# Two sequence mixers side by side: 2048-point transforms factored as 32 by 64 in place of 16 by 128

## The chip, the cores and the metric

The kernel runs on one core of a Trainium2 chip. Its engines are PE (matrix products; its weight loads are shown as PEld), DVE (elementwise work and scans), ACT (here mostly copies of PE's results out of PSUM), POOL (some integer work, and the issue of some transfers) and SP (the issue of the others). The metric is the device time of one execution in microseconds. Three runs of the kernel before gave 219.19, 219.22 and 219.26 us.

## What is computed

Two independent blocks take sequences of 2048 steps and 640 channels and write halves of one output row. Block A is a diagonal complex state-space layer, block B a gated long convolution (H3):

```python
# A: complex state per channel p
h = Lam_bar[None, :] * h + Bu[:, t, :]              # Bu = x @ B_bar.T, for t = 0 .. 2047
y = 2.0 * einsum("blp,dp->bld", hseq, Cmat).real + x * Dskip
# B
k_shift = sum over 4 taps of k_pad[:, t:t + S, :] * shift_k[:, 3 - t]
kv = k_shift * v
y = irfft(rfft(kv, 2S) * rfft(ssm_k, 2S))[:, :S] + kv * ssm_D
out = q * y
concatenate([A, B], axis=-1)                        # (1, 2048, 1280), bf16
```

## The kernel before

**Block A** works through four chunks c of 512 steps and, in each, five tiles j of 128 state channels; n = 5c + j. `z{n}` is ten matmuls of 512 columns (L356), `ze{n}` ACT's copy of the result. On DVE `rin{n}` turns the phase away with three tensor operations (`rotate`, L367 to L369), `sc{n}` scans the real and the imaginary part (L376) and `rout{n}` turns back (L367 to L369 again). `p{c}_{i}_{j}` projects tile j of 128 rows (L401, four matmuls of 320 columns; at j = 4 six more with the skip weights, L407), `yo` is ACT's copy (L411), `yd` the store (L415). `la` (POOL, L385) and `carry` (DVE, L390 to L392) hand the state to the next chunk.

**Block B** works through five groups G of 128 channels. `kT`, `vT` load k and v transposed, `dS` builds diagonal weights (L447), `tap` makes the short convolution on PE (L462), `kve` copies, `kv` multiplies by v on DVE (L473). `kvo` stores the product to DRAM and `kvs` loads it back as 128 rows of (channel in a set, coarse step) with one run of neighbouring steps each (`load_kv`, L478); `hs` loads the long filter in the same form, and `had` adds the skip coefficient to its first step (L444). Both go through a transform in two stages, `s1h`, `s1k` (L485) and `s2h`, `s2k` (L499 to L502), four parts each, each followed by ACT's copy out of PSUM (`s1he`, `s2ke` and so on; L490, L505). `y{G}_{hf}_{step}` multiplies the two spectra on DVE (L512, L514, L516 and L517). `inv` is the first stage back (L526 to L529), `zs` its copy (L533), `zt` a transposing DMA (L537), `fin` the last stage (L547), `obe` its copy (L554), `ob` the product with q on DVE (L559), `od` the store (L563). `qi` loads q.

The 2048-point transform (its odd frequencies, so that the convolution doesn't wrap) is factored as 16 by 128. `s1` is a contraction over 16 coarse steps and 8 channels of a set: 128 rows, of which two halves of 64 rows each make a matmul of their own, with 128 weight columns (the fine steps). `s2` contracts over the 128 fine steps, with four matmuls for the complex product, so that it needs a third table nGim beside Gre and Gim; the tables of the way back, Hre, Him and nHim, are made of them by transposing DMAs (`H0` to `H2`).

**Order.** `make_plan` declares some 650 tasks with engine, dependencies and the PSUM buffer that they take or give back; its costs are those of an earlier planning and have no effect on the run. `ORDER` (L728) is the finished order, written out as a list of task names with the PSUM buffer behind an @; tasks are issued in it, so each engine's queue is the subsequence of its own tasks, and each engine works strictly in that order. There are four PSUM buffers of 128 by 1024 f32.

Of the kernel before, what the change touches and what calls it, by code (L numbers as in the profile page):

```python
# [18 lines left out]
L = 2048  # L19
D = 640  # L20
# [42 lines left out]
class Kernel:  # L63


    def __init__(self, ctx, tc, out, ins):
# [28 lines left out]
        t("bitf", [128, 7], f32)  # L95
        for n, k in (("bits", 5), ("bsh", 4), ("ccol", 8)):
            t(n, [128, k], i32)
        t("r_mask", [128, 8])
        t("m_mask", [128, 8])
        t("sk_b", [128, NG, 2, 4])  # L100
        t("dcol_b", [128, 16 * NG])
        t("lo", [128, CW], i32)
        t("aph", [128, CW], f32)
        t("R", [128, 32, 4])
        t("Mq", [128, 2, 16, 8])
        for n in ("Gre", "Gim", "nGim", "Hre", "Him", "nHim"):
            t(n, [128, 16, 128])
# [21 lines left out]
        for n in ("h_st", "kv_st", "q0", "q1"):  # L129
            t(n, [128, 16, 128])  # L130
# [17 lines left out]
        self.gph = self.Y[:].rearrange("p a n -> p (a n)").bitcast(i32).rearrange("p (q a b) -> p q a b", q=4, a=4)
        self.tph = [q[:].rearrange("p a c -> p (a c)").bitcast(i32)[:, 512 * i:512 * i + 512] for q in (self.q0, self.q1) for i in range(2)]
        self.tph.append(self.h6[:].rearrange("p a n -> p (a n)").bitcast(i32))  # L150
        zf = self.Zt[:].rearrange("p i h b -> p (i h b)").bitcast(f32)
# [38 lines left out]
    def pool_consts2(self):  # L190
        g = self.nc.gpsimd
        g.iota(self.ccol[:], pattern=[[1, 8]], base=0, channel_multiplier=0)
        g.iota(self.ramp[:, 0:16], pattern=[[4, 16]], base=1, channel_multiplier=0)
        g.iota(self.ramp[:, 16:32], pattern=[[1, 16]], base=0, channel_multiplier=0)

    def dve_consts(self):
        v = self.nc.vector
        v.memset(self.hpi[:], PI / 2)
        v.memset(self.kTa[:, 0:PAD], 0.0)
        v.memset(self.dcol_b[:], 0.0)  # L200
        s = v.tensor_single_scalar
        s(out=self.ident[:], in_=self.ident[:], scalar=0.0, op=ALU.is_equal)
        s(out=self.bsh[:, 0:1], in_=self.pidx[:], scalar=19, op=ALU.logical_shift_left)
        for q in (1, 2):
            s(out=self.bsh[:, q:q + 1], in_=self.pidx[:], scalar=22 + q, op=ALU.logical_shift_left)
        v.tensor_scalar(out=self.bsh[:, 3:4], in0=self.pidx[:], scalar1=3, scalar2=None, op0=ALU.mult)
        s(out=self.bsh[:, 3:4], in_=self.bsh[:, 3:4], scalar=23, op=ALU.logical_shift_left)
        v.tensor_tensor(out=self.ident2[:], in0=self.ident[:, 0:64], in1=self.ident[:, 64:128], op=ALU.add)

    def dve_masks(self):  # L210
        v = self.nc.vector
        for i, (a, op0, c, op1) in enumerate(((4, ALU.arith_shift_right, 3, ALU.bitwise_and), (4, ALU.arith_shift_right, 2, ALU.logical_shift_left),
                                              (8, ALU.bitwise_and, 1, ALU.logical_shift_left))):
            v.tensor_scalar(out=self.bits[:, i:i + 1], in0=self.pidx[:], scalar1=a, scalar2=c, op0=op0, op1=op1)
        for i, c in ((3, 15), (4, 7)):
            v.tensor_single_scalar(out=self.bits[:, i:i + 1], in_=self.pidx[:], scalar=c, op=ALU.bitwise_and)
        v.tensor_copy(out=self.bitf[:, 0:5], in_=self.bits[:])
        for hf in range(2):
            v.tensor_scalar_add(out=self.bitf[:, 5 + hf:6 + hf], in0=self.bits[:, 1:2], scalar1=1.0 + 32 * hf)
        for m, c in ((self.r_mask, 0), (self.m_mask, 4)):  # L220
            v.tensor_scalar(out=m[:], in0=self.ccol[:], scalar1=self.bitf[:, c:c + 1], scalar2=None, op0=ALU.is_equal)

    def dve_phases(self):
        v = self.nc.vector
        r = self.r_ph.rearrange("p (k r) -> p k r", r=2)
        for i in range(2):
            v.tensor_scalar(out=r[:, :, i], in0=self.ramp[:, 0:16], scalar1=self.bitf[:, 3:4], scalar2=16.0 * i, op0=ALU.mult, op1=ALU.add)  # L227
            v.tensor_scalar(out=self.m_ph[:, 16 * i:16 * i + 16], in0=self.ramp[:, 16:32], scalar1=self.bitf[:, 5 + i:6 + i],
                            scalar2=self.bitf[:, 2:3], op0=ALU.mult, op1=ALU.add)
        both = self.rm_ph.rearrange("p n k -> p (n k)")  # L230
        v.tensor_single_scalar(out=both, in_=both, scalar=26, op=ALU.logical_shift_left)
# [4 lines left out]
    def dve_RM(self):  # L236
        v = self.nc.vector
        v.tensor_tensor(out=self.R[:], in0=self.r_cv.rearrange("p (k o) -> p k o", o=1).to_broadcast([128, 32, 4]),
                        in1=self.r_mask[:, 0:4].rearrange("p (o c) -> p o c", o=1).to_broadcast([128, 32, 4]), op=ALU.mult)
        v.tensor_scalar_mul(out=self.m_cv, in0=self.m_cv, scalar1=1.0 / L)  # L240
        for hf in range(2):
            v.tensor_tensor(out=self.Mq[:, hf],
                            in0=self.m_cv[:, 16 * hf:16 * hf + 16].rearrange("p (a o) -> p a o", o=1).to_broadcast([128, 16, 8]),
                            in1=self.m_mask[:].rearrange("p (o c) -> p o c", o=1).to_broadcast([128, 16, 8]), op=ALU.mult)
# [85 lines left out]
    def pool_G(self, q):  # L330
        g = self.nc.gpsimd
        flat = lambda n: self.gph[:, n].rearrange("p a b -> p (a b)")
        if q == 0:
            g.iota(self.gph[:, 0], pattern=[[4, 4], [64, 128]], base=1, channel_multiplier=0)
        g.tensor_tensor(out=flat(q), in0=flat(0), in1=self.bsh[:, q:q + 1].to_broadcast([128, 512]), op=ALU.add if q else ALU.mult)

    def act_G(self, g):
        ph, s = self.gph[:, 2 * g:2 * g + 2].rearrange("p q a b -> p (q a b)"), slice(8 * g, 8 * g + 8)
# [79 lines left out]
    def load_dcol(self):  # L418
        self.nc.sync.dma_start(out=self.dcol_b[0:128:16, :], in_=self.B_ssm_D.rearrange("(i c) -> c i", c=8))
# [19 lines left out]
    def load_h(self, G):  # L439
        self.nc.sync.dma_start(out=self.h_st[:], in_=self.B_ssm_k[128 * G:128 * G + 128, :].rearrange(  # L440
            "(i c) (a b) -> (c a) i b", c=8, b=128))

    def pool_skip(self, G):
        self.nc.gpsimd.tensor_tensor(out=self.h_st[:, :, 0], in0=self.h_st[:, :, 0], in1=self.dcol_b[:, 16 * G:16 * G + 16], op=ALU.add)  # L444
# [33 lines left out]
    def load_kv(self, G):  # L478
        self.nc.gpsimd.dma_start(out=self.kv_st[:], in_=self.kvd[G].rearrange("(i c) (a b) -> (c a) i b", c=8, b=128))

    def pe_s1(self, st, q, ps):
        for i in range(4):
            for r in range(2):
                rows = slice(64 * r, 64 * r + 64)
                self.nc.tensor.matmul(ps[:, r, 128 * i:128 * i + 128], lhsT=st[rows, 4 * q + i, :],  # L485
                                      rhs=self.R[rows].rearrange("p k c -> p (k c)"), start=True, stop=True,
                                      tile_position=(64 * r, 0))

    def act_s1(self, As, q, ps):
        self.nc.scalar.copy(out=As[:, :, 32 * q:32 * q + 32].rearrange("p k (i r c) -> p k i r c", i=4, r=2),  # L490
                            in_=ps[:].rearrange("p r (i k c) -> p k i r c", i=4, k=32))

    def pe_s2(self, As, q, ps):
        mm = self.nc.tensor.matmul
        for i in range(4):
            k1 = 4 * q + i
            cs = slice(i * 128, (i + 1) * 128)
            re, im = As[:, 2 * k1, :], As[:, 2 * k1 + 1, :]
# [20 lines left out]
    def pe_inv(self, q, ps):  # L519
        mm = self.nc.tensor.matmul  # L520
        psf = ps[:].rearrange("p a n -> p (a n)")
        for i in range(4):
            k1 = 4 * q + i
            yre, yim = self.Y[:, 0, 128 * k1:128 * k1 + 128], self.Y[:, 1, 128 * k1:128 * k1 + 128]
            o_re, o_im = psf[:, 256 * i:256 * i + 128], psf[:, 256 * i + 128:256 * i + 256]
            mm(o_re, lhsT=self.Hre[:, k1, :], rhs=yre, start=True, stop=False)  # L526
            mm(o_re, lhsT=self.nHim[:, k1, :], rhs=yim, start=False, stop=True)  # L527
            mm(o_im, lhsT=self.Him[:, k1, :], rhs=yre, start=True, stop=False)  # L528
            mm(o_im, lhsT=self.Hre[:, k1, :], rhs=yim, start=False, stop=True)  # L529

    def act_zs(self, q, ps):
        k0 = 8 * (q % 2)
# [297 lines left out]
```

## Time and profile before

| | |
|---|---|
| median of three runs | 219.22 us |
| the profiled execution | 219.12 us |
| its span in the profile, first to last instruction and transfer | 217.4 us |
| DVE from the first rotation (rin0) to the end of the last (rout19) | 16.15 to 204.88 us |
| transposing and plain loads and stores on the hardware queue | 99336 packets, 24.68 MB, 60.5% of 16 engines |
| POOL's queue of transfers | 2592 packets, 9.31 MB, 15.6% |

The profile's page gives busy times of each engine, a strip of the span in 40 slices, the chain of work that ended last, and groups of instructions by source line (L...) with their count, busy time and mean length. "A<-B" is output and inputs; "64*128" behind a matmul is rows by columns of the weights in PE's array. A matmul's recorded length includes its way through the array, some 0.2 us; how fast a series runs is read from the distance of the starts (its pitch).

### The profile page before, as it was taken

Reading aid. Unit: us, or ns where it says so; the run is one execution under the profiler, and the core shown is the slowest. Engines: PE = TensorE matmul, PEld = TensorE weight load, DVE = VectorE, ACT = ScalarE, POOL = GpSimd, SP = SyncE. Lnnn points to the kernel's source line nnn. Section 1 sums busy time; section 2 is a strip of 40 time slices with the busy share of each in tenths; the row PEclk is TensorE's granted clock in tenths of the full one; section 3 lists DMA queues with packets and bytes.
Section 4 is the critical chain, followed back from the end, with each engine's and each line's share of the span. In section 5 each row is a group of like instructions: output and inputs, shape, how many; then the busy total and the mean of one; then the engine's idle time right before and its main releaser. Section 6 shows DMA issues by size and latency. Waiting matters only on the chain.

```text
span 217.4 us, 5287 instructions
## 1 busy us (share of the span) xinstructions
PE 192.9 (89%) x2223; PEld 136.4 (63%) x2235; DVE 201.6 (93%) x301; ACT 169.7 (78%) x199; POOL 40.1 (18%) x66
## 2 busy tenths in 40 slices
PE   2698479469989999999999999999999999999890
PEld 1243237366545586775699745699477995887580
DVE  7899999999999999999999999999999999999920
ACT  2689998999867589996699967799999995672061
POOL 8560120001030102400223020134131002101010
PEclk9999859979999999999999999999999999999999
DMA  6699999980929892955988890487996049639168
GB/s 146 111 197 169 209 253 212 213 169 12 175 107 217 204 191 90 241 146 100 216 232 210 182 190 6 98 184 161 216 204 163 3 29 225 190 77 196 60 163 151
DMA packets 101982, 34.33 MB, mean 158 GB/s; under 512 B 99014, under 2 KB 99782, under 8 KB 101958
## 3 DMA queue, kind: packets, MB, share of 16 engines
q1 hardware_dynamic: 99336, 24.68, 60.5%
q0 software_dynamic: 2592, 9.31, 15.6%
q8 instruction: 17, 0.28, 0.5%
q14 instruction: 7, 0.06, 0.1%
q10 hardware_dynamic: 30, 0.00, 0.0%
HBM read 8.21 MB, written 7.86 MB: 74 GB/s over the span
## 4 chain that ended last, share of the span: by engine, by line
DVE 88%; issue 6%; PE 3%; ACT 0%; DVEq 0%; POOL 0%; POOLq 0%; ACTq 0%
DVE u L376 22%; DVE rot_p L367 12%; DVE rot_x L368 11%; DVE w L369 6%; DVE pw_x L514 5%; DVE h L369 4%; DVE Y L512 4%; DVE Cs L314 4%; DVE Y L516 3%; DVE vT L473 3%; DVE Y L517 3%; PE ps L401 2%; DVE q L559 2%; DVE diagS L447 1%; DVE rot_p L227 1%
## 5 line engine op out<-in xcount | busy, mean ns | idle before, releaser
L401 PE MATMUL ps<-Cs,h 128*128 128x320 bf16 x320 | 53.6, 300 | 2.4 <-DVE Cs L314 1.3
L356 PE MATMUL ps<-xT,BT 128*128 128x512 bf16 x188 | 47.9, 394 | 2.0 <-DMA BT<-in_A_B_re_dram 0.5
L401 PEld LDWEIGHTS <-h 128*128 128x128 bf16 x320 | 27.9, 98 | 15.2 <-issue 2.1
L376 DVE TENSOR_TENSOR_SCAN u<-rr,carry,w 128x512 bf16<-128x512 f32 x30 | 36.9, 1270 | 0.4
L356 PEld LDWEIGHTS <-BT 128*128 128x128 bf16 x200 | 19.4, 101 | 25.1 <-issue 4.9
L641 ACT CAST z<-ps 128x1024 bf16<-128x1024 f32 x20 | 20.2, 1009 | 7.4 <-PE ps L356 6.1
L411 ACT CAST yo<-ps 128x640 bf16<-128x640 f32 x16 | 11.2, 700 | 16.4 <-PE ps L407 16.1
L505 ACT CAST Xs<-ps 128x1024 bf16<-128x1024 f32 x20 | 20.6, 1055 | 1.5 <-PE ps L502 1.3
L490 ACT CAST As_h<-ps 128x1024 bf16<-128x1024 f32 x20 | 20.0, 1029 | 2.2 <-PE ps L485 2.2
L490 ACT CAST As_kv<-ps 128x1024 bf16<-128x1024 f32 x20 | 19.5, 1024 | 2.6 <-PE ps L485 2.6
L499 PE MATMUL ps<-As_kv,Gre 128*128 128x128 bf16 x80 | 18.3, 228 | 3.1 <-ACT As_kv L490 3.1
L533 ACT CAST zz<-ps 128x1024 bf16<-128x1024 f32 x20 | 20.3, 1065 | 0.7 <-PE ps L529 0.7
L505 ACT CAST Hf<-ps 128x1024 bf16<-128x1024 f32 x20 | 20.1, 1043 | 0.4 <-ACT yo L411 0.4
L385 POOL CAST last<-h 128x2 f32<-128x2 bf16 x15 | 7.0, 473 | 63.7 <-DVE h L369 61.2
L500 PEld LDWEIGHTS <-nGim 128*128 128x128 bf16 x160 | 16.1, 100 | 4.1 <-issue 3.5
L501 PE MATMUL ps<-As_kv,Gim 128*128 128x128 bf16 x80 | 18.3, 228 | 0.0
L502 PE MATMUL ps<-As_kv,Gre 128*128 128x128 bf16 x80 | 18.3, 228 | 0.0
L500 PE MATMUL ps<-As_kv,nGim 128*128 128x128 bf16 x80 | 18.3, 228 | 0.0
L499 PE MATMUL ps<-As_h,Gre 128*128 128x128 bf16 x80 | 17.5, 219 | 0.5 <-ACT Hf L505 0.5
L526 PE MATMUL ps<-Y,Hre 128*128 128x128 bf16 x80 | 17.5, 219 | 0.0
L527 PE MATMUL ps<-Y,nHim 128*128 128x128 bf16 x80 | 17.5, 219 | 0.0
L528 PE MATMUL ps<-Y,Him 128*128 128x128 bf16 x80 | 17.5, 219 | 0.0
(136 smaller groups left out, 513.3 us busy)
## 6 DMA issues: line engine op xcount, KB each, us to landing
h_st<-in_B_ssm_k_dram SPq DMA_DIRECT2D x5, 512.0 KB, 4.8
kv_rows<-vT POOLq DMA_DIRECT2D x5, 512.0 KB, 4.3
kv_st<-kv_rows POOLq DMA_DIRECT2D x5, 512.0 KB, 6.7
q<-in_B_q_dram SPq DMA_DIRECT2D x5, 512.0 KB, 6.7
out_dram<-q POOLq DMA_DIRECT2D x4, 512.0 KB, 5.8
out_dram<-yo POOLq DMA_DIRECT2D x12, 160.0 KB, 4.6
out_dram<-yo SPq DMA_DIRECT2D x4, 160.0 KB, 3.6
out_dram<-q SPq DMA_DIRECT2D x2, 256.0 KB
```

What stands on the lines that cost most here:

```text
L356: self.nc.tensor.matmul(ps[:, r, :], lhsT=self.BT[:, r, k, j * 128:(j + 1) * 128], rhs=xT[:, k, :], start=(k == 0), stop=(k == NT - 1))
L367: tt(out=self.rot_p[:], in0=self.tabs[:, j, 0:1, :].to_broadcast([128, 2, CW]), in1=v, op=ALU.mult)
L368: tt(out=self.rot_x[:], in0=self.tabs[:, j, 1:3, :], in1=v[:, ::-1, :], op=ALU.mult)
L369: tt(out=out, in0=self.rot_p[:], in1=self.rot_x[:], op=op)
L376: self.nc.vector.tensor_tensor_scan(out=self.u[:, r, :], data0=rb, data1=self.w[:, r, :], initial=ini, op0=ALU.mult, op1=ALU.add)
L401: mm(ps[:, b, 0:320], lhsT=h[:, r, ts], rhs=self.Cs[:, r, j, c0:c0 + 320], start=(j == 0 and r == 0), stop=False)
L490: self.nc.scalar.copy(out=As[:, :, 32 * q:32 * q + 32].rearrange("p k (i r c) -> p k i r c", i=4, r=2), in_=ps[:].rearrange("p r (i k c) - ...
L499: mm(ps[:, 0, cs], lhsT=self.Gre[:, k1, :], rhs=re, start=True, stop=False)
L500: mm(ps[:, 0, cs], lhsT=self.nGim[:, k1, :], rhs=im, start=False, stop=True)
L505: self.nc.scalar.copy(out=dst[:, :, o:o + 512], in_=ps[:])
L533: self.nc.scalar.copy(out=self.Zs[:, :, q // 2, k0:k0 + 8, :].rearrange("p i k c -> p k i c"), in_=ps[:].rearrange("p a n -> p (a n)").rea ...
L641: A(f"ze{n}", "ACT", EV, [f"z{n}"] + old, lambda ps, n=n: K.nc.scalar.copy(out=K.zt(n)[:], in_=ps[:]), give=f"z{n}")
```

## The change

The transform is factored as 32 by 64. Loads bring sets of 4 channels with 32 coarse steps, runs of 64 steps (128 bytes) in place of 128 steps (256 bytes). `s1` contracts over all 128 rows and has 64 weight columns; one matmul makes the real part in PSUM rows 0 to 63, a second the imaginary part in rows 64 to 127, each in its own half of the array's columns. Real and imaginary part then lie in the 128 rows of the contraction of `s2`, so that one matmul of 64 weight columns does what two did; two frequencies go to the two halves of the columns. `inv` puts two frequencies into the two halves of the rows. `fin` uses halves of the columns again. nGim, nHim and their making (`nG0`, `nG1`, `H2`) go; `hs`, `kvs`, `qi` and `od` move runs of 128 bytes (the last group's `od` 64), and `qi` and `od` are two DMAs each.

```diff
-            "(i c) (a b) -> (c a) i b", c=8, b=128))
+            "(i c) (a b) -> (c a) i b", c=4, b=64))          # load_h, load_kv
     def pe_s1(self, st, q, ps):
+        for i in range(8):
+            for r in range(2):
+                self.nc.tensor.matmul(ps[64 * r:64 * r + 64, i // 4, 128 * (i % 4):128 * (i % 4) + 128], lhsT=st[:, 8 * q + i, :],
+                                      rhs=self.R[:, r], start=True, stop=True, tile_position=(0, 64 * r))
-        for i in range(4):
-            for r in range(2):
-                rows = slice(64 * r, 64 * r + 64)
-                self.nc.tensor.matmul(ps[:, r, 128 * i:128 * i + 128], lhsT=st[rows, 4 * q + i, :],
-                                      rhs=self.R[rows].rearrange("p k c -> p (k c)"), start=True, stop=True,
-                                      tile_position=(64 * r, 0))
     def pe_s2(self, As, q, ps):
...
-            mm(ps[:, 0, cs], lhsT=self.Gre[:, k1, :], rhs=re, start=True, stop=False)
-            mm(ps[:, 0, cs], lhsT=self.nGim[:, k1, :], rhs=im, start=False, stop=True)
-            mm(ps[:, 1, cs], lhsT=self.Gim[:, k1, :], rhs=re, start=True, stop=False)
-            mm(ps[:, 1, cs], lhsT=self.Gre[:, k1, :], rhs=im, start=False, stop=True)
+            for r, G in enumerate((self.Gre, self.Gim)):
+                for h in range(2):
+                    self.nc.tensor.matmul(ps[64 * h:64 * h + 64, r, 128 * i:128 * i + 128], lhsT=G[:, 4 * q + i, 64 * h:64 * h + 64],
+                                          rhs=As[:, 8 * q + 4 * h + i, :], start=True, stop=True, tile_position=(0, 64 * h))
     def pe_inv(self, q, ps):
...
+            for r, H in enumerate((self.Hre, self.Him)):
+                for h in range(2):
+                    rows = slice(64 * h, 64 * h + 64)
+                    self.nc.tensor.matmul(ps[:, h, 128 * i:128 * i + 128], lhsT=H[rows, k, :], rhs=self.Y[rows, r, 128 * k:128 * k + 128],
+                                          start=(r == 0), stop=(r == 1), tile_position=(64 * h, 0))
     def act_zs(self, q, ps):
-        self.nc.scalar.copy(out=self.Zs[:, :, q // 2, k0:k0 + 8, :].rearrange("p i k c -> p k i c"),
-                            in_=ps[:].rearrange("p a n -> p (a n)").rearrange("p (k i c) -> p k i c", k=8, i=16))
+        self.nc.scalar.copy(out=self.Zs[:, :, 8 * q:8 * q + 8, :],
+                            in_=ps[:].rearrange("p a n -> p (a n)").rearrange("p (k i c) -> p i k c", k=8, i=32))
     def load_q(self, G):
+        for h in range(2):
+            o = 128 * G + 64 * h
+            self.nc.sync.dma_start(out=self.qt(G)[64 * h:64 * h + 64], in_=self.rows_of(self.q2, o, o + 64))
     def pe_fin(self, hf, ps):
...
-            for kh in range(2):
-                self.nc.tensor.matmul(psf[:, 128 * i:128 * i + 128], lhsT=self.Zt[:, 8 * hf + i, kh, :],
-                                      rhs=self.Mq[:, kh].rearrange("p a c -> p (a c)"), start=(kh == 0), stop=(kh == 1))
+            for r in range(2):
+                for h in range(2):
+                    self.nc.tensor.matmul(psf[64 * h:64 * h + 64, 128 * i:128 * i + 128], lhsT=self.Zt[:, 16 * h + 8 * hf + i, 64 * r:64 * r + 64],
+                                          rhs=self.Mq[:, r], start=(r == 0), stop=(r == 1), tile_position=(0, 64 * h))
     def dve_ob(self, G, hf):
-        q = self.qt(G)[:, :, 64 * hf:64 * hf + 64]
+        q = self.qt(G)[:, :, 32 * hf:32 * hf + 32]
```

`ORDER` is replaced as a whole. DVE's tasks of some chunks, and the end of the list:

```
before  rin5 sc5 rout5 y0_0_2 y0_1_1 rin6 sc6 rout6 y0_1_2 kv2_0 kv2_1 rin7 sc7 rout7 dS3 rin8 sc8 rout8 rin9
after   rin5 dS2 sc5 y0_0_0 rout5 y0_0_1 rin6 y0_0_2 sc6 y0_1_0 rout6 kv2_1 kv2_0 rin7 y0_1_1 sc7 dS3 rout7 y0_1_2 rin8

before  sc19 zt4 rout19 ob3_1 p3_2_2 p3_1_3 p3_0_2 ob3_0 p3_2_3 p3_0_3 p3_1_4 yd2_2 yo3_1 yd2_1 p3_0_4 fin4_0 yo3_0 od3 p3_3_0
        obe4_0 ob4_0 yd3_0 fin4_1 p3_3_1 p3_2_4 p3_3_2 p3_3_3 yd3_1 p3_3_4 obe4_1 ob4_1 yo3_2 od4_0 yd3_2 od4_1 yo3_3 yd3_3
after   fin4_0 obe4_0 p3_0_3 p3_2_2 p3_2_3 yd2_2 ob4_1 p3_3_0 rout19 p3_0_4 p3_2_4 p3_3_1 yo3_0 p3_1_4 od4_1 ob4_0 yd3_0 yo3_2
        yo3_1 p3_3_2 yd3_2 od4_0 p3_3_3 yd3_1 p3_3_4 yo3_3 yd3_3
```

At the head the tasks `vec`, `rho` (DVE) stand behind the phases `pp` before, and ahead of them after; `dc2` and `pp` (masks and phases, L214 to L231) have fewer and other small instructions.

More of the change, by code (lines that the diff above doesn't have):

```diff
@@ L217, in dve_masks @@
[L217 to L221, printed above, removed]
+        v.tensor_scalar(out=self.bits[:, 3:4], in0=self.pidx[:], scalar1=2, scalar2=2, op0=ALU.arith_shift_right, op1=ALU.logical_shift_left)
@@ L223, in dve_phases @@
     def dve_phases(self):
         v = self.nc.vector
[L225 to L229, printed above, removed]
+        for m in range(2):
+            for i in range(2):
+                v.tensor_scalar(out=self.rm_ph[:, m, 32 * i:32 * i + 32], in0=self.ramp[:, 32 * m:32 * m + 32], scalar1=self.bitf[:, 2 + m:3 + m],
+                                scalar2=-32.0 * i, op0=ALU.mult, op1=ALU.add)
@@ L230, in dve_phases @@
         both = self.rm_ph.rearrange("p n k -> p (n k)")
-        v.tensor_single_scalar(out=both, in_=both, scalar=26, op=ALU.logical_shift_left)
+        v.tensor_single_scalar(out=both, in_=both, scalar=25, op=ALU.logical_shift_left)
     def act_RM(self):
@@ L614, in make_plan @@
         A(f"G{g}", "ACT", 2.75, [f"gp{2 * g}", f"gp{2 * g + 1}", "rr", "dc"], lambda g=g: K.act_G(g))
-        A(f"nG{g}", "DVE", 0.4, [f"G{g}"], lambda g=g: K.minus(K.nGim[:, 8 * g:8 * g + 8, :], K.Gim[:, 8 * g:8 * g + 8, :]))
-    Gs = ["G0", "G1", "nG0", "nG1"]
+    Gs = ["G0", "G1"]
     A("warm", "PE", 0.427 * 8, ["~bt0", "~bt1"], lambda ps: K.pe_warm(8, ps), take="warm", give="warm")
@@ L680, in make_plan @@
         dma(f"kvo{G}", "POOL", 0.6, 2.2, 1.4, [f"kv{G}_0", f"kv{G}_1"], lambda G=G: K.store_kv(G))
-        dma(f"kvs{G}", "POOL", 1.16, 2.5, 4.3, [f"kvo{G}"] + ([f"s1k{G - 1}_{q}" for q in range(4)] if pre else []), lambda G=G: K.load_kv(G))
+        dma(f"kvs{G}", "POOL", 1.16, 3.6, 4.3, [f"kvo{G}"] + ([f"s1k{G - 1}_{q}" for q in range(4)] if pre else []), lambda G=G: K.load_kv(G))
         for q in range(4):
-            A(f"s1h{G}_{q}", "PE", 4 * P128 + 0.05, [f"had{G}", "dRM"], lambda ps, q=q: K.pe_s1(K.h_st, q, ps), take=f"s1h{G}_{q}")
+            A(f"s1h{G}_{q}", "PE", 8 * P128 + 0.05, [f"had{G}", "dRM"], lambda ps, q=q: K.pe_s1(K.h_st, q, ps), take=f"s1h{G}_{q}")
             A(f"s1he{G}_{q}", "ACT", EV, [f"s1h{G}_{q}"] + ([f"s2h{G - 1}_{x}" for x in range(4)] if pre else []),
@@ L691, in make_plan @@
         for q in range(4):
-            A(f"s1k{G}_{q}", "PE", 4 * P128 + 0.045, [f"kvs{G}", "dRM"], lambda ps, q=q: K.pe_s1(K.kv_st, q, ps), take=f"s1k{G}_{q}")
+            A(f"s1k{G}_{q}", "PE", 8 * P128 + 0.05, [f"kvs{G}", "dRM"], lambda ps, q=q: K.pe_s1(K.kv_st, q, ps), take=f"s1k{G}_{q}")
             A(f"s1ke{G}_{q}", "ACT", EV, [f"s1k{G}_{q}"] + ([f"s2k{G - 1}_{x}" for x in range(4)] if pre else []),
@@ L725, in make_plan @@
     return p
 ORDER = """
-B0 pc ldldt pc2 dc ldlim gp0 ldlre vt@0 dc2 pp vec exp x0 bt1@1 bt0@2 rho bte1 Fi gp1 ldsk kT0 gp2 gp3 warm@0 bte0 B1 dS0 rr
-z0@2 tp0 trig1 tp3 num rec aRM gam vT0 tap0_0@0 tap0_1@1 tab0 tp1 dRM ze0 tab1 tp2 tn0 B2 rin0 tab2 z1@2 kve0_0 sc0 dcol rout0
-tn1 z2@0 kve0_1 ze1 tp4 G1 hs0 kv0_1 kv0_0 G0 tn2 kvo0 CT0 had0 ze2 dS1 rin1 s1h0_0@2 nG1 sc1 rout1 s1h0_3@1 s1h0_2@3 s1he0_0
-s1he0_3 s1he0_2 nG0 s1h0_1@0 rin2 s1he0_1 tab3 la1 sc2 z3@2 kvs0 z4@3 ze3 s2h0_2@0 s2h0_0@1 ze4 tab4 s2h0_3@2 tn3 CT1 rout2
@@ L762 @@
-sc19 zt4 rout19 ob3_1 p3_2_2 p3_1_3 p3_0_2 ob3_0 p3_2_3 p3_0_3 p3_1_4 yd2_2 yo3_1 yd2_1 p3_0_4 fin4_0@2 yo3_0 od3 p3_3_0@1
-obe4_0 ob4_0 yd3_0 fin4_1@3 p3_3_1 p3_2_4 p3_3_2 p3_3_3 yd3_1 p3_3_4 obe4_1 ob4_1 yo3_2 od4_0 yd3_2 od4_1 yo3_3 yd3_3
+ldldt pc B0 pc2 dc ldlim ldlre vt@0 dc2 bt0@1 vec exp bte0 x0 rho ldsk bt1@0 gp0 pp B1 rr Fi warm@2 aRM bte1 z0@0 kT0 trig1
+gp1 gp2 dRM gp3 tp0 tp1 tp4 tab0 ze0 tab1 z1@2 B2 ze1 num vT0 dS0 rec tap0_1@2 tn0 gam rin0 tp3 tn1 sc0 rout0 tap0_0@0 tp2
+z2@1 tab2 tn2 hs0 G1 kve0_0 rin1 dS1 sc1 dcol rout1 kve0_1 z4@2 la1 tab4 had0 lddsk CT0 tab3 s1h0_0@0 ze2 z3@1 ze4 CT1 kv0_0
```

193 lines of the change are left out of this document (88 added, 105 removed).

## The prediction

> **What bounds the kernel now.** I read the page's busy rows and chain first, then a table by stretches, then two timelines.
>
> ```profile
> span 217.4 us, 5287 instructions
> ...
> PE 192.9 (89%) x2223; PEld 136.4 (63%) x2235; DVE 201.6 (93%) x301; ACT 169.7 (78%) x199; POOL 40.1 (18%) x66
> ...
> DVE 88%; issue 6%; PE 3%; ACT 0%; DVEq 0%; POOL 0%; POOLq 0%; ACTq 0%
> ```
>
> DVE is the bound and PE is close behind. The table by stretches (columns: length, then busy time of PE, PEld, DVE, ACT, POOL; granted clock, DMA share, GB/s) says where:
>
> ```profile
> 16.10:60.00 43.90, 33.43 (x312) 20.78 (x312) 43.07 (x61) 41.70 (x50) 3.82 (x8) 0.88 1.01 177
> 60.00:110.00 50.00, 48.45 (x583) 32.33 (x585) 49.03 (x66) 38.90 (x44) 8.48 (x14) 1.00 0.78 167
> 110.00:160.00 50.00, 49.68 (x659) 37.73 (x662) 48.99 (x68) 44.92 (x51) 11.93 (x18) 1.00 0.75 168
> ```
>
> From its first rotation at 16.15 to the last (rout19, done at 204.88) DVE hardly rests, and from 60 on PE hardly does either. So the time has three parts: a head of 16.15, a DVE stream of 188.7, a tail of 12.5. Less PE work shortens none of them by itself. What shortens the stream is fewer or tighter DVE instructions. The timeline of DVE shows that they are not tight:
>
> ```profile
> 44.04 0.69 DVE L369 TENSOR_TENSOR h<-rot_p,rot_x 128x1024 bf16<-128x1024 bf16 x1
> 44.83 0.69 DVE L367 TENSOR_TENSOR rot_p<-tabs,z 128x1024 bf16<-128x1024 bf16 x1
> ...
> 46.16 0.69 DVE L369 TENSOR_TENSOR w<-rot_p,rot_x 128x1024 bf16<-128x1024 bf16 x1
> 46.88 2.34 DVE L376 TENSOR_TENSOR_SCAN u<-rr,w 128x512 bf16<-128x512 f32 x2
> ...
> 50.59 0.69 DVE L369 TENSOR_TENSOR h<-rot_p,rot_x 128x1024 bf16<-128x1024 bf16 x1
> 51.20 1.80 DVE L314 SCALAR_TENSOR_TENSOR Cs<-Cs,g,Zt 128x640 bf16<-128x640 bf16 x2
> ```
>
> The same multiply-add L369 is followed after 0.61 us by an independent instruction (50.59 to 51.20), after 0.72 to 0.73 by the scan that reads it (46.16 to 46.88), and after 0.79 from 44.04 (of which the profile puts 0.06 to DVE's own queue). A dependent neighbour costs 0.12 us.
>
> **The change, part by part**, against the profiled execution (219.12 us, which is span 217.4 plus 1.72; the median of the three runs is 219.22, 0.10 above it).
>
> *DVE's queue.* The new ORDER puts another task between the steps of a chunk. From rin0 on, I count neighbours of which the second reads the first (rin-sc, sc-rout, rout-rin, the steps of y, the two cs of one j): 14+15+9+4+3 = 45 before, 2+3+2 = 7 after. 38 x 0.12 = **-4.5**. nG0 and nG1 go (L328 on nGim, 0.34 to the next instruction each): **-0.7**. Nine ob tasks, not six, stand ahead of rout19, 0.60 each (pitch of L559 pairs): **+1.8**, taken from the tail. I price ob's 64-byte runs as now; the other end is twice that, +5. Stream: 188.7 - 3.4 = 185.3 if DVE waits for nobody.
>
> *Head.* Fi now waits behind L227 to L231 (3.67 to 7.1), and POOL idles 2.36 us for it (9.06, table product L319). Beside POOL's products DVE's small instructions take about 1 us (L227 1080 ns, L286 1005) and 0.17 otherwise. The new order runs vec and rho ahead of the phases, so Fi and tp0 come earlier; the same small instructions still stand before rin0. Between 0 and POOL's 2.4 idle us, I take **-1.5**: rin0 at 14.6.
>
> *PE, work.* A full matmul of 128 columns has a pitch of 0.056 (sixteen L547 take 1.06, the last one 0.22 of it). Two matmuls of half the rows already share that slot:
>
> ```profile
> 158.53 0.71 PE L401 MATMUL ps<-Cs,h 128*128 128x320 bf16 x4
> 159.17 0.40 PE L485 MATMUL ps<-R,h_st 64*128 64x128 bf16 x8
> 159.50 0.58 PE L401 MATMUL ps<-Cs,h 128*128 128x320 bf16 x3
> ```
>
> Eight L485 take 0.40, 0.22 of it the last one's length: four slots of about 0.056, not eight. Per group of channels the slots were s1 32, s2 128, inv 64, fin 32; if half-width matmuls share a slot too, they become 64, 64, 32, 32. 5 x (256 - 192) x 0.056 = -17.9 of PE's work.
>
> *PE, changes of shape.* In the same fence L401 has a pitch of 0.136, so L485 could start at 159.07 and starts at 159.17; and L401 follows the last pair (159.35) by 0.15 instead of 0.056. Each change of tile shape costs 0.095. Counting neighbours in ORDER by shape (full; s1, s2 and fin; inv; tap) gives 69 before and 139 after: 70 x 0.095 = +6.7. PE nets -11, from 192 to 181, while the order it runs in is new.
>
> *The new wait.* From rin5 to rin12 the new ORDER gives PE 23 s1, 17 s2 and 9 inv (0.45 each), 2 fin (0.90), 8 z (2.16), 24 projections at 0.54 and 6 at 0.83, 6 taps (1.72), 69.4, and 74 changes, 7.0: 76.4 us. DVE's tasks in that stretch are 66.8. Before, the stretch held 61.8 against 60.4 and DVE did not wait. So PE falls up to 9.6 us behind, less what it is ahead at rin5; y and kv, which read its results, then stop DVE and all behind them (scans, rotations). Bounds 0 and +9.6; I take the middle, **+4.7**. Without it the forecast would be 211.3.
>
> *Tail.* The timeline's end now:
>
> ```profile
> 204.19 0.69 DVE L369 TENSOR_TENSOR h<-rot_p,rot_x 128x1024 bf16<-128x1024 bf16 x1
> ...
> 204.94 0.45 PE L401 MATMUL ps<-Cs,h 128*128 128x320 bf16 x2 [1.08 <-DVE h L369]
> ...
> 212.46 0.69 ACT L411 CAST yo<-ps 128x640 bf16<-128x640 f32 x1 [1.26 <-PE ps L407]
> 212.49 0.44 SPq L563 DMA_DIRECT2D out_dram<-q  x1
> 213.17 0.89 SPq L415 DMA_DIRECT2D out_dram<-yo  x1
> ```
>
> Behind rout19 PE now runs two fin and 0.36 of waiting for zz; the new ORDER leaves it four p_4 (0.83) and three projections (0.54): 4.95. With 0.06 to its start, 0.33 for drain and hand-over, 0.69 for yo and 3.6 for the store (DMA list, SP's yo stores; 4.2 now, right behind a q store) that is 9.6 instead of 12.5: **-2.9**.
>
> *Transfers, ACT, POOL.* hs, kvs, qi, od double their runs at half the size. In the trace's packets the 4096 runs of 128 bytes of today's last q stores took 13 ns of an engine each, those of 256 bytes 21.7 on average: 3.3 us against 2.8 per 512 KB over 16 engines, hidden behind loads issued a group ahead; one H transpose less gives 2.8 back where the DMA share is 1.01. POOL's issue goes from 1.17 to about 1.8 (0.55 for 128 runs, 1.17 for 2048), od to two of 1.17; behind them stand la and yd, and POOL idles 61 us for h. SP issues q twice (0.4 to 0.8). ACT's evacuations keep their 1024 elements and their pitch of 0.90 (zs and obe now in runs of 4 elements, as s1 has today at the same pitch); a tenth more on all of them would be 11 us of ACT's 48 idle ones. All at 0, between nothing and the dear cases below.
>
> **Sum.** 14.6 + 185.3 + 4.7 + 9.6 = 214.2 span, + 1.72 = **216.0 us**.
>
> **Rivals.**
>
> *Half-width matmuls do not share a slot (slower).* No row shows two column tiles that both use all 128 rows: the pairs of L462 and L485 differ in their rows. Then 1600 matmuls of s1, s2 and fin take 0.056 each, not 0.028: +44.8 on PE, whose 181 become 226. With the start near 7.5, some 10 idle us before 60 (43.9 - 33.4) and 4.6 behind the last matmul the span is 248, the time 250. It decides from a small surplus on: a nanosecond per pair is 0.8 us on PE in all and 0.35 in the critical stretch, about 0.5 on the end, so the gain of 3.1 is gone at a slot of 62 ns. For it: that gap. Against it: the 64-column loads of L462 begin in pairs like its matmuls, and 128-column loads of 98 ns already overlap at a pitch of 56.
> The Trainium skill speaks for this rival: TensorEngine Tiling (Array Packing), Restrictions and Gotchas, says that column tiling excludes Fast Weight Load, and TensorE: Matmul & The Clock Gate, Part 3, that weight loads overlap running matmuls only when the row group differs. By that page's Part 2, P / 1.2, a 64-column load is 53 ns, two in a row 107, nearly the 112 of an unshared pair, and the sum would be an estimated 246. The trace's overlapping full-array loads speak against the second rule. Chance 0.14.
>
> *Dear pairs or changes.* A slot of 60 to 75 ns, a change of 0.15 (139 x 0.055 = 7.6, most of it on a PE that sets the pace), or evacuations slowed by 8-byte runs: 219.5 to 228, near 222. Chance 0.18.
>
> *Dear short runs.* If 128 bytes cost as much as 256 (21.7 ns), each of some twenty transfers takes 5.5 us, not 2.8, and the chain kv, kvo, kvs, s1k of five groups lengthens by 2.7 each; a third of it shown on DVE is +4.5: 220.5. Today's last stores speak against it. Chance 0.05.
>
> *No wait.* PE's lead covers the stretch: 211.3, with a better head 210. Chance 0.12.
>
> *The forecast*, 213 to 219: 0.51.
>
> **From these the numbers.** A measurement of this kernel tells 0.2%, 0.45 us, from no change. Faster: 0.12 and most of 0.51, 0.60; within 0.2%: 0.06; slower: 0.34. The range of 8 in 10 leaves out the unshared case and the best of no wait: 211 to 228. The likeliest case by itself: 213 to 219.
>
> **What would show it.** Right: s2 with sixteen matmuls in about 0.64 (eight slots and the drain); rin0 near 14.6; scans that follow an independent task; DVE's waits for PE or ACT of 3 to 7 us between 60 and 150; about 10 us behind rout19. Wrong: sixteen s2 in 1.1; PE's busy share at 95% with DVE's below 85%; ob at 1.1 us; waits for kv_st or h_st on PE.

## The result, and the profile after

The changed kernel takes **217.05 us** (median of four runs, 216.07 to 217.7); the kernel before 219.23 on the same chip. The ratio is 0.9897, 95% interval 0.9883 to 0.9912: faster by one per cent. The forecast was 216.0. The profiled execution took 217.26. Some runs of the kernels below were slowed (longer, at a lower granted clock): medians and ratios leave them out, and a kernel with a single run left has no ratio.

The page of the changed kernel, its busy row and its chain:

```profile
span 215.5 us, 6250 instructions
...
PE 185.1 (86%) x2702; PEld 117.8 (55%) x2715; DVE 196.4 (91%) x295; ACT 169.8 (79%) x199; POOL 50.6 (24%) x70
...
PE 65%; ACT 13%; issue 10%; DVE 6%; POOL 3%; DMA 1%; ACTq 0%; DVEq 0%; POOLq 0%
```

By busy time little has changed: both engines have a few us less, and DVE still has more than PE. The chain is another one: it was DVE for 88% of the span, now it is PE for 65%. The table by stretches (columns as in the prediction) shows how close both are:

```profile
60.00:110.00 50.00, 49.62 (x762) 31.13 (x765) 49.59 (x68) 43.63 (x49) 10.12 (x15) 1.00 0.95 171
110.00:160.00 50.00, 47.72 (x872) 32.48 (x873) 46.09 (x62) 45.77 (x52) 10.32 (x14) 1.00 0.66 139
```

From 110 to 160 DVE has 46.09 of work in 50; before it had 48.99. Of the other 3.9 us 3.5 are waits, and the kernel before had none between rin0 and rout19. The waits (engine and line, what it waited for: us in total, times, longest):

```profile
DVE Y L493 <- PE ps L506: 1.8, 1, 1.8
DVE Y L493 <- ACT Xs L486: 0.9, 1, 0.9
...
DVE vT L460 <- ACT lo L456: 0.7, 1, 0.7
DVE Cs L301 <- ACT Zt L297: 0.5, 1, 0.5
```

With 0.18 for a z these are 4.1 us between rin0 and rout19: a product of spectra waits from 115.06 to 116.89 for `inv` (L506) to have read the Y of the group before, others for ACT's copies of PE's results.

PE's timeline shows what the new matmuls cost:

```profile
60.52 2.32 PE L343 MATMUL ps<-xT,BT 128*128 128x512 bf16 x9
62.77 0.25 PE L482 MATMUL ps<-As_kv,Gre 128*64 128x128 bf16 x2
...
62.91 0.22 PE L482 MATMUL ps<-As_kv,Gre 128*64 128x128 bf16 x2
62.96 0.22 PE L482 MATMUL ps<-As_kv,Gim 128*64 128x128 bf16 x2
...
63.63 0.22 PE L482 MATMUL ps<-As_kv,Gim 128*64 128x128 bf16 x2
63.79 0.45 PE L388 MATMUL ps<-Cs,h 128*128 128x320 bf16 x2
```

Each L482 row with x2 is a pair of column halves; the pairs follow at 0.05 to 0.06 (by the start times of single matmuls 0.003 within a pair and 0.052 to the next, a slot of 0.055), so a pair shares a slot, although each half contracts over all 128 rows. Into the pairs and out of them stands a gap. In the start times of single matmuls, a change of shape makes a pitch of 0.136 (behind L388) into 0.229 on the way in and one of 0.056 into 0.152 on the way out: 0.093 and 0.096. The first pair behind a change takes 0.08 instead of 0.055 (62.77 to 62.85).

Where the 1.9 us of the two profiled executions come from: the head gives 0.1 (rin0 at 16.04, before 16.15), the stream from rin0 to the end of rout19 takes 189.5 instead of 188.7 (3.3 less of work, 4.1 more of waits), and the tail 9.95 instead of 12.5. All that arrives at the end is the tail. Behind rout19 PE has 5.1 us left, and SP's last issues of yo end at 212.35 (rows of PE, ACT and SP):

```profile
205.60 0.45 PE L388 MATMUL ps<-Cs,h 128*128 128x320 bf16 x2 [0.86 <-DVE h L356]
...
210.41 0.30 PE L394 MATMUL ps<-diagD,xT 128*128 128x64 bf16 x3
210.79 0.69 ACT L398 CAST yo<-ps 128x640 bf16<-128x640 f32 x1 [1.22 <-PE ps L394]
210.33 2.02 SPq L402 DMA_DIRECT2D out_dram<-yo  x2
```

### The profile page after: what moved, and what is told of

Read it like the earlier page. It is cut to its first block, busy times and chain, and to the rows that moved or that the text cites. A ratio compares the mean times of both kernels' runs of the same rounds, so it can differ in the third digit from the quotient of the medians.

```text
span 215.5 us, 6250 instructions
## 1 busy us (share of the span) xinstructions
PE 185.1 (86%) x2702; PEld 117.8 (55%) x2715; DVE 196.4 (91%) x295; ACT 169.8 (79%) x199; POOL 50.6 (24%) x70
## 4 chain that ended last, share of the span: by engine, by line
PE 65%; ACT 13%; issue 10%; DVE 6%; POOL 3%; DMA 1%; ACTq 0%; DVEq 0%; POOLq 0%
PE ps L388 19%; PE ps L343 16%; PE ps L482 9%; PE ps L471 7%; PE ps L449 4%; PE ps L506 4%; ACT As_h L475 3%; PE ps L529 2%; PE ps L394 2%; POOL q L306 2%; ACT Zt L297 1%; ACT Xs L486 1%; ACT As_kv L475 1%; DMA rows<-in_A_Lambda_re_dram 1%; ACT Hf L486 1%
## 5 line engine op out<-in xcount | busy, mean ns | idle before, releaser
L388 PE MATMUL ps<-Cs,h 128*128 128x320 bf16 x320 | 55.6, 301 | 1.0 <-DVE h L356 0.9
L388 PEld LDWEIGHTS <-h 128*128 128x128 bf16 x320 | 26.1, 98 | 14.2 <-DVE h L356 1.2
L482 PEld LDWEIGHTS <-Gre 128*64 128x64 bf16 x320 | 17.8, 111 | 13.1 <-issue 12.5
L372 POOL CAST last<-h 128x2 f32<-128x2 bf16 x15 | 9.8, 670 | 63.8 <-DVE h L356 63.8
L449 PE MATMUL ps<-kTa,diagS 64*64 64x512 bf16 x80 | 14.4, 430 | 4.8 <-DVE Cs L301 3.1
L482 PEld LDWEIGHTS <-Gim 128*64 128x64 bf16 x320 | 18.3, 111 | 0.0
L471 PE MATMUL ps<-RM,h_st 128*64 128x128 bf16 x320 | 12.7, 226 | 6.4 <-POOL h_st L431 6.1
L471 PEld LDWEIGHTS <-h_st 128*64 128x64 bf16 x320 | 10.0, 112 | 10.9 <-POOL h_st L431 6.6
L482 PE MATMUL ps<-As_h,Gre 128*64 128x128 bf16 x160 | 11.9, 229 | 3.4 <-ACT As_h L475 3.1
L449 PE MATMUL ps<-kTb,diagS 64*64 64x512 bf16 x80 | 14.8, 430 | 0.0
L493 DVE TENSOR_TENSOR Y<-Xs,Hf 128x2048 bf16<-128x2048 bf16 x10 | 12.2, 1217 | 2.8 <-PE ps L506 1.8
L356 DVE TENSOR_TENSOR h<-rot_p,rot_x 128x1024 bf16<-128x1024 bf16 x20 | 13.8, 692 | 0.9
```

The lines of the kernel that those rows point to most:

```text
L356: tt(out=out, in0=self.rot_p[:], in1=self.rot_x[:], op=op)
L388: mm(ps[:, b, 0:320], lhsT=h[:, r, ts], rhs=self.Cs[:, r, j, c0:c0 + 320], start=(j == 0 and r == 0), stop=False)
L449: self.nc.tensor.matmul(ps[cols, half, :], lhsT=self.diagS[rows, turned, j, :], rhs=src[rows, t0:t0 + 512], start=(j == 0), stop=(j == 3), ...
L471: self.nc.tensor.matmul(ps[64 * r:64 * r + 64, i // 4, 128 * (i % 4):128 * (i % 4) + 128], lhsT=st[:, 8 * q + i, :], rhs=self.R[:, r], sta ...
L482: self.nc.tensor.matmul(ps[64 * h:64 * h + 64, r, 128 * i:128 * i + 128], lhsT=G[:, 4 * q + i, 64 * h:64 * h + 64], rhs=As[:, 8 * q + 4 * ...
L493: tt(out=Y[:, :, hs], in0=Xs[:], in1=self.Hf[:, 0:1, hs].to_broadcast([128, 2, 1024]), op=ALU.mult)
```

## The experiments

My theory: the factoring frees PE, the new ORDER spends that on a tighter DVE queue, and the two only work together; what is left of the new kernel is PE's pace. Rivals: the ORDER alone makes the gain, the factoring alone makes it, or pairs do not really share.

**1 and 2. Each half of the change alone.** `old_fact_new_order` is the kernel before with the new ORDER; nG0, nG1 and H2, which that factoring needs, are put behind G0, G1 and H1. `new_fact_old_order` is the changed kernel with the old ORDER, these three left out.

> The 16 by 128 factoring in the new ORDER (nG0, nG1 and H2 put back behind G0, G1 and H1). My theory: the new ORDER takes some 4.5 us of dependent neighbours off DVE, but PE must keep up with it, and with the old factoring PE's queue is 10 us longer (192 against 181): PE sets the pace, DVE waits 8 to 14 us for it, and the time is 223 to 228 us, slower than before. Rival, the ORDER alone made the gain: 217 us or less. In either case DVE's stream without its waits should be near 186 us.

> The 32 by 64 factoring in the old ORDER (without nG0, nG1, H2). My theory: DVE keeps its 45 dependent neighbours, so that from its first rotation to the end of the last it needs 188 us as before less 0.7 for nGim, and waits for nobody before the last q; the tail gains nothing but some tenths: 217.5 to 218.7 us. Rival, the factoring alone made the gain by shorter PE work: 217.0 us or less.

| median, us (ratio to before, 95%) | old ORDER | new ORDER |
|---|---|---|
| 16 by 128 | 219.23 | 229.22 (1.0449 to 1.048) |
| 32 by 64 | 224.15 (1.0216 to 1.025) | 217.05 (0.9883 to 0.9912) |

Either half by itself makes the kernel slower. The first goes as my theory said, a little beyond its 223 to 228, and an ORDER that gains by itself (217 or less) is refuted. Each ORDER was found for its own factoring, so the two mixed kernels show what belongs together and not what either half could be worth in an ORDER of its own. The old factoring in the new ORDER has 16.4 us of waits in DVE's stream. The largest of them, and its stretches:

```profile
DVE Y L512 <- ACT Xs L505: 7.2, 4, 2.7
DVE Y L512 <- PE ps L529: 5.4, 2, 4.6
...
60.00:110.00 50.00, 48.96 (x605) 33.42 (x602) 47.41 (x64) 41.91 (x46) 8.01 (x13) 1.00 0.83 163
110.00:160.00 50.00, 48.43 (x650) 37.82 (x649) 39.86 (x55) 40.00 (x44) 7.18 (x14) 1.00 0.65 135
```

PE is full, and DVE has only 39.86 of work in the second 50 us: the queue that the new ORDER tightens on DVE is one that the old transforms cannot feed. Without its waits the stream takes 202.5 - 16.4 = 186.1, 2.6 less than before, so the tightening itself is the ORDER's and works with the old factoring too. The shorter tail is the ORDER's as well: 8.9 here.

The new factoring in the old ORDER is a miss for both theories. Its stream is as expected (rin0 at 16.0, no waits, rout19 done at 204.49), so less PE work shortens nothing by itself. But its tail takes 17.6 us, not 12.5. SP's timeline there:

```profile
207.12 2.08 SPq L402 DMA_DIRECT2D out_dram<-yo  x2
209.30 4.18 SPq L546 DMA_DIRECT2D out_dram<-q  x2
213.57 1.43 SPq L402 DMA_DIRECT2D out_dram<-yo  x1
215.06 2.12 SPq L546 DMA_DIRECT2D out_dram<-q  x2
217.27 1.00 SPq L402 DMA_DIRECT2D out_dram<-yo  x1
```

Before, an od4 store (L563, 128-byte runs) occupied SP for 0.38 and 0.44. The same store in two DMAs of 64-byte runs occupies it for 4.18 and 2.12, and the last yo, copied at 213.20, is issued at 217.27. The new ORDER issues the first od4 at 203.57, ahead of all yo stores of the last chunk.

**3. The last store in longer runs.** `tail_one_store` is kernel 2 with one task for the last group's product:

```diff
-            for hf in range(2):
-                dma(f"od{G}_{hf}", "SP", ..., [f"ob{G}_{hf}"], lambda G=G, hf=hf: K.store_ob(nc.sync, G, 32 * hf, 32 * hf + 32))
+            dma(f"od{G}", "SP", ..., [f"ob{G}_0", f"ob{G}_1"], lambda G=G: K.store_ob(nc.sync, G, 0, 64))
```

> The new factoring in the old ORDER (224.15 us), with the product of the last group stored by one task behind both ob4, in runs of 128 bytes (two DMAs), not by two tasks in runs of 64 bytes (four DMAs). Theory (the runs of 64 bytes hold SP's queue, 4.18 and 2.12 us for od4, and the last yo stores stand behind them): the last yo store is issued when it is ready, near 213.2, and the end is 4 to 5 us earlier: 218.8 to 220.5 us. Rival (the tail is long because PE and ACT hand the last yo over late in that order): the time stays within 1 us of 224.15.

Measured 220.45 (220.19 to 220.78; ratio to before 1.0041 to 1.0073), 3.7 less: inside the theory's times, at their upper end. SP's timeline:

```profile
207.61 4.48 SPq L402 DMA_DIRECT2D out_dram<-yo  x3
212.20 2.56 SPq L546 DMA_DIRECT2D out_dram<-q  x2
```

The last yo, copied at 213.69, now stands behind one store of 2.56 us (212.20 to 214.76) and is issued at 214.81. That is still late by 1.1, and the tail is 14.0: these 1.1 to 1.5 us are what remains above 219.23. The edit does two things at once, longer runs and one store less in the way of yo (yd3_2 goes ahead of it); it does not tell them apart.

**4. Pairs that follow each other in the same half of the columns.** `unshared_s2` runs the loops of `s2` in another order, the same matmuls otherwise:

```diff
-        for i in range(4):
-            for r, G in enumerate((self.Gre, self.Gim)):
-                for h in range(2):
+        for h in range(2):
+            for i in range(4):
+                for r, G in enumerate((self.Gre, self.Gim)):
```

> The new kernel with the loops of s2 turned, so that all eight matmuls of one half of the columns come before those of the other and no two neighbours can share a slot. Sixteen L482 then take 16 slots of 0.055, 0.44 us more in each of 40 s2: 17.8 us on PE. My theory, PE sets the pace between 60 and 160 us: 229 to 233 us. Rival, PE's work lies beside DVE's and is hidden: 217 to 219 us.

Measured 223.77, one run: slower by 6.7, not by 12 or more, and not by nothing. (Its granted clock, 0.969, is no lower than the 0.957 to 0.964 of the changed kernel's runs.) PE's timeline of one `s2`:

```profile
66.14 0.22 PE L482 MATMUL ps<-As_h,Gim 128*64 128x128 bf16 x1
66.19 0.25 PE L482 MATMUL ps<-As_h,Gre 128*64 128x128 bf16 x2
...
66.36 0.25 PE L482 MATMUL ps<-As_h,Gim 128*64 128x128 bf16 x2
66.45 0.22 PE L482 MATMUL ps<-As_h,Gre 128*64 128x128 bf16 x1
```

The first half's matmuls run alone at 0.056 (rows x1), but its last four run beside the first four of the other half (rows x2), although they stand four apart in the program: the ninth matmul starts at 66.198, beside the fifth (66.192) and ahead of the sixth (66.248), so PE does not start its queue strictly in order here. The sixteen take 0.67 from first start to last, not the 0.42 of the pairs and not the 0.84 of fifteen unshared slots. At most 40 x 0.25 = 10 us of PE's work (its busy time grows by 8.1, to 193.2), of which 6.7 reach the end; DVE's waits grow from 4.1 to 11.1. Sharing is shown, and so is PE as the bound; my size for it was wrong because I took sharing to need neighbours.

**5. More changes of shape.** `more_shapes` puts one full-shape matmul of a single column into the middle of each `s1`, where its result is written over later: 80 more changes and 40 short matmuls.

> The new kernel with one matmul of one column in the full shape ahead of the fifth pair of each s1 (its result is overwritten), so that there are 80 more changes of shape, 7.6 us of PE at 0.095 each and 1 us for the matmuls. My theory, changes cost what the trace of before shows and PE sets the pace over half of the span: 220 to 223 us. Rival, a change is hidden while DVE works: 217 us as without it. A third possibility, the change costs more beside column tiles (0.2): 225 us or more.

Measured 222.29 (221.96 to 222.89), ratio 1.0149, 1.0129 to 1.0169: 5.2 more, with 9.0 us of waits instead of 4.1 and PE's busy time at 192.3 instead of 185.1. In the trace an `s1` by itself takes 0.648 from its first start to its last, without the insertion 0.418: 0.23 for two changes and the short matmul, 40 x 0.23 = 9.2 on PE. That is a little more than the 7.6 and 1 of the expectation, since the first pair behind a change is slow, and 5.2 of it reach the end.

**6 to 8. Other ORDERs.** `searched_new` has DVE's and PE's tasks rearranged from rin0 on, with 112 changes of shape instead of 139; `searched_new_one` differs from it by the store of experiment 3, issued by POOL; `searched_old` is the same for the old factoring.

> The new factoring in another ORDER with 112 changes of tile shape, not 139, in which PE's work is spread so that DVE should not wait; the two stores od4 of 64-byte runs stand close together on SP's queue, ahead of three yo stores. Theory (what is left of the new kernel is PE's pace in 37 to 151, and the stores of 64-byte runs hold SP): the stream loses its 4.1 us of waits, but the tail takes 12 to 16 us, not 10: 214.5 to 219 us. Rival A (stores do not hold SP where nothing else is in the way): 211 to 213.5. Rival B (PE is no bound, the waits come from the order of DVE's own tasks): the stream keeps 3 us or more of waits.

> As searched_new, with the product of the last group stored by one task in runs of 128 bytes, issued by POOL, so that SP's queue holds yo stores only behind it. Theory: 2 to 6 us below searched_new, 210.5 to 214 us (217.26 less 4.1 of waits, and a tail as now). Rival (the tail is not the stores): within 1 us of searched_new.

> The old factoring (16 by 128) in an ORDER found in the same manner, with 55 changes of shape, not 69, and fewer dependent neighbours on DVE. Theory (the old factoring loses to PE's 192 us as soon as DVE's queue is tightened): 215 to 219.5 us, a gain of at most 4 and above the searched order of the new factoring by 3 or more. Rival (the factoring is worth nothing in itself, the order is all): within 1.5 us of searched_new_one.

Measured 231.5 (229.9 and 233.12; ratio 1.0461 to 1.066), 230.82 (one run, no ratio) and 220.94 (1.0058 to 1.0102). The first is a failure that none of the theories had. Waits in it, of PE and of DVE:

```profile
PE ps L471 <- POOL h_st L431: 7.8, 1, 7.8
PE ps L343 <- DMA xT<-in_A_x_dram: 6.5, 2, 5.5
...
DVE Cs L301 <- ACT Zt L297: 7.3, 3, 5.2
DVE rot_p L354 <- ACT z L623: 3.3, 1, 3.3
```

rin5 comes at 73.4, in the changed kernel at 60.9, and DVE waits 11.6 us ahead of it instead of 0.7. The longest of these waits, 5.2 until 59.98, goes back, by the profile, to a load: PE stands 5.5 us for the second part of x, ACT 6.9 for the z that needs it, and DVE for ACT. PE's 7.8 for the long filter (POOL's addition to it waits for the skip coefficients) are 6.1 in the changed kernel too. Behind rin5 it is faster: 134.5 to rin19, not 137.5. What the order wins there is lost ahead of it, where the DMA share is 0.93 even in the changed kernel. `searched_new_one` tells nothing of the store, since the same loss covers it. That the old factoring gets no better than 220.94 agrees with the theory but proves little: one order, found in one way.

**9 and 10. The ORDER kept up to rin5.** `mid_search_c` and `mid_search_b` keep the order of the tasks up to rin5 (with other PSUM buffers) and rearrange the rest.

> The changed kernel with its ORDER kept word for word up to rin5 (60.9 us), so that loads and head stay as they are, and rearranged behind it: 110 changes of tile shape, not 139, and PE's tasks placed so that no DVE task should wait. Theory (behind 60 the changed kernel waits for PE: 3.9 of its 4.1 us of waits lie there, and the chain is PE's): rin5 stays near 61, the waits behind it fall below 1.5 us, rout19 ends at 201 to 203.5, a tail of 10 to 12: 213 to 217 us. Rival (what failed in searched_new was not the loads ahead of rin5, but the packing of the stream itself): rin19 comes at 198 or later and the time is 217 us or more.

> As mid_search_c, another arrangement behind rin5: 117 changes, and one of the two od4 stores early, the other ahead of the last three yo stores. Theory: 213 to 217 us, the tail 10 to 11.5. Rival: 217 us or more.

Measured 217.2 (215.75, 215.94, 218.51 and 218.52; ratio 0.987 to 0.9953) and 218.7 (0.9961 to 0.9994). By their medians both miss the 213 to 217, though two runs of the first lie inside. In `mid_search_b` the stream behaves: rin5 at 61.0, rin19 at 197.0 instead of 198.4, waits behind rin5 of 2.0 instead of 3.5 (I had asked for less than 1.5). The tail, at 12.2 instead of 9.95, takes more than that back:

```profile
202.59 5.00 SPq L546 DMA_DIRECT2D out_dram<-q  x2
207.64 1.18 SPq L402 DMA_DIRECT2D out_dram<-yo  x1
208.92 2.34 SPq L546 DMA_DIRECT2D out_dram<-q  x2
```

The last three yo stores follow at 211.35, and ACT's last yo copies wait 2.79 and 1.02 for the stores ahead of them to free their buffers.

**11. The head.** `head_late` is the changed kernel with dRM and gam moved from ahead of rin0 to right behind it.

> The changed kernel with two DVE tasks of the head, the products for the tables of block B (dRM, 1.79 us beside POOL's integer products, behind a wait of 0.78 for ACT) and the factors gamma (gam), moved from ahead of rin0 to right behind it, where POOL is done. Both theories: rin0 at 13.3 to 14.3, not 16.04, and the two tasks cost DVE about 1.7 behind it, so that DVE's queue is 0.7 to 1.5 us ahead at sc0. If DVE's stream still sets the end, as the sum of the prediction takes it: 0.7 to 1.5 below the changed kernel, 215.6 to 216.4 us. If PE sets the pace from about 40 on: DVE's waits behind 37 grow by what was gained, and the time is within 0.4 of 217.05.

Measured 217.2 (ratio 0.9886 to 0.9943), as the changed kernel. But the test did not do what it was made for: rin0 starts at 13.5, and the scan behind it at 18.08, in the changed kernel at 18.17. DVE's timeline:

```profile
12.53 1.03 DVE L315 TENSOR_SCALAR tabs<-tabs 128x512 bf16<-128x512 bf16 x1
13.48 1.52 DVE L354 TENSOR_TENSOR rot_p<-tabs,z 128x1024 bf16<-128x1024 bf16 x1
```

Beside POOL's integer products (until 14.5) L315 takes 1.03 instead of 0.25 and L354 1.52 instead of 0.69. The slow time beside POOL is only filled with other instructions, and the two tasks come later. So DVE was never ahead, and whether a lead there would reach the end stays open.

**12. The best of these.** `mid_search_d` is `mid_search_b` with the last product stored by one task of 128-byte runs on POOL.

```diff
-ob4_1 rout19 ob4_0 od4_1 p3_0_3 ... yo3_3 od4_0 yd3_2 yd3_1 yd3_3
+ob4_1 rout19 ob4_0 od4 p3_0_3 ... yo3_3 yd3_2 yd3_1 yd3_3
```

> As mid_search_b, with the last group's product stored by one task in runs of 128 bytes, issued by POOL (idle there) right behind ob4_0, in place of the two tasks of 64-byte runs that held SP for 5.00 and 2.34 us and made ACT's last yo copies wait for the stores of the ones before. Theory (64-byte stores hold SP's queue, and that alone makes the tail 12.2 and not 9.9): the last yo is stored as soon as it is copied, the tail is 9.5 to 10.5, and the time is 1.5 to 2.7 us below mid_search_b: 216.1 to 217.3 us. Rival (the tail is PE's and the stream's gain is lost in the clock): within 0.7 of 218.8.

Measured **216.24** (215.53 to 217.13), ratio 0.9857, 0.9837 to 0.9876; 2.4 below `mid_search_b`, and its interval lies wholly below that of the changed kernel. The tail is 10.3. SP now issues yo stores only (four, from 206.86 on). Run length, number of stores and issuing engine change together here; which of them it is stays open.

Kernels 10 and 12 also gave a test that I had not planned. Their ORDER is the same up to the tail, but in the profiled run of 12 the granted clock fell for 3.4 us. The stretch 73 to 77 in `mid_search_b`:

```profile
73.00:77.00 4.00, 4.00 (x80) 2.84 (x76) 4.00 (x5) 3.59 (x4) 0.00 (x0) 1.00 1.02 216
```

and in `mid_search_d`:

```profile
73.00:77.00 4.00, 4.00 (x43) 2.75 (x44) 4.00 (x5) 3.84 (x4) 0.00 (x0) 0.57 1.08 215
```

PE loses 4 x 0.43 = 1.7 us of work there. DVE is full in both. Fourteen us later DVE waits at L493 for 2.5 us in `mid_search_d` and for 0.9 in `mid_search_b`: 1.6 of PE's 1.7 come out as a wait. The instructions of DVE and ACT from 61 to 70 start 0.5 earlier in `mid_search_d`; behind the fall ACT's copies come 1.1 later, and DVE's instructions stay 0.5 earlier up to that wait and are 1.1 later behind it, so the wait is this delay and nothing that stood ahead of it. PE sets the pace in this stretch.

## Why the prediction was right, and where not

- **DVE's queue, right.** The stream without its waits takes 185.4, forecast 185.3. Experiments 1 and 2 give two of its parts: the ORDER by itself takes off 2.6 (188.7 to 186.1), forecast 4.5 less 1.8; the factoring, with nG0 and nG1 gone, 0.8 in the new ORDER (186.15 to 185.36) and 0.3 in the old one (188.73 to 188.45), forecast 0.7.
- **The new wait, right in its mechanism, its size in part luck.** 4.1 us, forecast 4.7, the middle of bounds of 0 and 9.6. Of it 2.6 lie between rin5 and rin12, where I had put all of it (1.82 and 0.75), 0.93 behind it and 0.66 ahead of it. The mechanism is shown by experiments 4 and 5 and by the fall of the clock: more PE time turns into DVE waits. One sign of being wrong was there, too: PE waits 6.1 us for h_st, until 31.05; DVE's waits ahead of rin5 are 0.7 all the same.
- **The tail, right.** 9.95, forecast 9.6.
- **The head, wrong.** This is the step of the sum that failed: "rin0 at 14.6", a gain of 1.5; measured 16.04, a gain of 0.1. The cost that it left out is DVE's own work beside POOL, which the earlier Fi does not shorten. Its rows in the changed kernel:

```profile
4.60 0.17 DVE L242 COPY vec<-ps 128x15 f32<-128x15 f32 x1 [0.78 <-PE ps L239]
...
9.57 1.79 DVE L230 TENSOR_TENSOR RM<-rot_p,rm_mask 128x256 bf16<-128x256 f32 x2 [0.78 <-ACT rot_p L159]
```

  vec runs ahead of the phases but waits for its rows, the phases (L220, 1.5) still stand ahead of Fi, and Fi is ready at 8.62 instead of 8.81. RM, which stood behind POOL's products before (R and Mq, 0.28 and 0.49), now stands beside them, with a wait. Experiment 11 says more: the start of rin0 was the wrong thing to forecast. DVE's work in the head, slowed beside POOL, sets when the stream can go on.
- **PE's slots and changes, right; their sum not.** Pairs share (0.055 against 0.056), a change costs 0.093 to 0.096 against 0.095. But PE's busy time fell to 185.1, not 181. The slow first pair is one part that the sum left out: 54 changes to column halves x 0.024 = 1.3. PE's work at half the clock is another: 10.1 us of its busy time, before 8.8 (the clock from 16 to 60 was 0.84 against 0.88), some 0.6. The other 2 us are open.
- **Transfers at nothing: right in this ORDER only.** 128-byte packets took 13 ns of a DMA engine, 64-byte ones 8.7, so the DMA engines lost little by the short runs. What I had not priced is SP's queue: a pair of 64-byte stores holds it for up to 5.00 us. The new ORDER issues them where little stands behind them; elsewhere, taking them out of the way was worth 2.4 (10 against 12) and 3.7 us (2 against 3).
- **The rivals.** "Half-width matmuls do not share a slot" is refuted by the pitch of the pairs. The weight loads of 64 columns last 0.110 us each in the trace, not the 53 ns of that rival's estimate, and still two of them fit into 0.055. The rule cited from the Trainium skill (TensorE: Matmul & The Clock Gate, Part 3), that loads overlap running matmuls only when the row group differs, does not hold here: both halves use all rows. The exclusion of Fast Weight Load (TensorEngine Tiling (Array Packing), Restrictions and Gotchas) may be seen in the 0.110 against 0.098 for a full load, and costs no slot. "Dear changes" is refuted by 0.095, "no wait" by 4.1 us of waits.

PE lost slots worth 17.9 us by my count, took on 6.7 of changes, and its busy time fell by 7.8; the kernel is faster by one per cent only, because DVE's stream of 188.7 lost only 3.3 of work and took on 4.1 of waits, with PE still full from 60 to 110. The forecast's net came out 1.3 us low on the profiled execution: 1.4 of head and 0.35 of tail, less 0.6 of waits.

## What to carry to other kernels

A change of the algorithm and the order of its instructions are one change: try the two halves apart before you credit either, for here each alone is slower (1.0465 and 1.0233, the second still 1.0057 when its stores of short runs are out of the way) and both together faster (0.9897). A freed engine gives time only where another order can use it; look at the chain and not at the busy shares for who sets the pace then. Where runs in a transfer get shorter, look at what stands behind it on its issuing queue, above all in the last 10 us.

## What was not expected of the hardware

- Two halves of PE's columns overlap even when the matmuls for them stand four apart in the program (experiment 4: 0.67 for sixteen, not 0.84), and PE then starts the ninth matmul ahead of the sixth.
- Two DMAs of 64-byte runs (128 KB each) took SP 1.65 to 5.00 us to issue, two of 128-byte runs (256 KB each) 2.56 on SP and 2.21 on POOL, one of 128-byte runs in the kernel before (256 KB, L563) 0.38 to 0.44. So it is no price per run: 2048 runs of 128 bytes take 0.4 in one kernel and 1.3 in another (there over 64 partitions, not 128, and behind other stores). What decides it was not measured.
- A fall of the granted clock to a half for 3.4 us came out on DVE, 14 us later, as 1.6 us of wait (experiment 12).
